# First batch of a windowed-attention and ELU kernel: masks and transposes moved to TensorE, softmax by whole heads, weights converted two halves at a time

## The chip, the cores and the metric

The kernel runs on one core of one Trainium2 chip. The metric is the device time of one execution in microseconds; the median of three runs before the change is 927.81 us (927.35 to 928.17).

## What is computed

Attention with a window, for 8 batches of 8 heads with 576 positions of 64 numbers, and then two large matrix products with an ELU between them, on 4608 tokens. Everything is float32 to the caller except that the weights arrive as float64.

```
scores = q @ k^T / 8
heads 0-3: keys 0..31 positions back        heads 4-7: 0..127 back, every 4th
attn   = exp(scores - max) / (sum + 1e-9)   out = attn @ v
x = out, all heads side by side             (4608 x 512)
h = x @ w_in        (512 x 2048)
g = h if h > 0 else exp(h) - 1
result = g @ w_out  (2048 x 512)
```

The host lays q, k and v out by pairs of heads and reorders the positions, so that each block of 32 queries sees only its own and the preceding 32 keys. So one pair of heads has 12 units (2 heads x 6) of 96 queries by 64 keys.

## The kernel before, in words

**Stages.** Attention of batch 0 runs first. Then come 9 chunks of 512 tokens. A chunk has 16 steps `f`; each multiplies by 128 columns of `w_in` (`gemm1`, L210), applies the ELU (`elu`, L221) and, two steps later (`LAG`), multiplies by 128 rows of `w_out` (`gemm2`, L237). Attention of batch `c + 1` is strewn over the steps of chunk `c` in eight portions. Chunk 0 multiplies in plain float32; from chunk 1 on each product is three matmuls of float32r parts (`xh`, `xl`, `wh`, `wl`).

**Attention of a pair of heads** (`attention`, L139): 36 small matmuls for the scores; for each of 12 units one custom VectorE (DVE) instruction that adds the mask and takes the maximum (L160) and one ScalarE (ACT) exponential with an accumulated sum (L163); on DVE the sum plus 1e-9, reciprocal and product (L164 to L166); six DVE transposes of 32x32 blocks into `pt` (L173); 12 matmuls with v; two ACT copies into `x32` (L185 or L188). In batch 0 all four pairs are first taken up to the product, then each is transposed and multiplied with v. GpSimd (POOL) does the product from batch 2 on.

**Weights** (`convert`, L81): a half is 128x512 numbers of `w_in` or `w_out`, 512 KB in float64. ACT takes the magnitude of the high words (L88), DVE does four integer operations (L89 to L96). There are 32 halves, in the order in which the steps need them; the first product of chunk 0 needs the first half, and every step needs two more. In chunk 1 the halves are split into `wh` and `wl` (`split_w`, L98). In the beginning a one-element POOL copy (L78) holds the loads of later halves back.

**What sets the order.** Matmuls keep program order on TensorE (PE), whose records all carry L109, the line of the helper `mm`. The other engines' order is drawn up by the scheduler of the tile framework, from its own model of time; an `issue_after` only puts instructions behind another one on the same engine. All loads and stores go through one queue, SyncE's (SP), in order. PSUM has 8 banks: two for `h_ps`, four for `o_ps`, two for attention (`a_ps`).

Of the kernel before, what the change touches and what calls it, by code (L numbers as in the profile page):

```python
# [9 lines left out]
F32 = mybir.dt.float32  # L10
# [7 lines left out]
WINDOW, DIL = 32, 4  # L18
# [14 lines left out]
NM = 5  # L33
AHEAD = 8
NR = NF
NE = 8
# [4 lines left out]


def _mask_of(dil, n):
    return n % 3 if dil else 3 + (n > 0)
# [3 lines left out]
def body(ctx: ExitStack, tc: tile.TileContext, q, k, v, masks, w_in, w_out, out):  # L48
# [10 lines left out]
    mask_sb = const.tile([QB, NM, 2 * G], F32, name="mask_sb")  # L59
# [3 lines left out]
    early = [wst.tile([P, 2 * DM], F32, name=f"r{NR - NE + i}") for i in range(NE)]  # L63
# [3 lines left out]
    raw, full = [None] * 2 * NF, [None] * 2 * NF  # L67
# [5 lines left out]
    def load_w(j, after=None):  # L73

        i = need[j]
        raw[i] = wst.tile([P, DM], I64, name=f"r{j % NR}")
        if after is not None:
            nc.gpsimd.tensor_copy(out=raw[i].bitcast(F32)[:QB, 0:1], in_=after[:, 0:1])  # L78
        nc.sync.dma_start(out=raw[i], in_=(w_in, w_out)[i % 2][i // 2])

    def convert(j):  # L81

        i = need[j]
        u = raw[i].bitcast(U32).rearrange("p (c two) -> p c two", two=2)
        lo, hi = u[:, :, 0], u[:, :, 1]

        e = wst.tile([P, DM], F32, name="w_e", bufs=2)
        nc.scalar.activation(out=e, in_=hi.bitcast(F32), func=AF.Abs)  # L88
        nc.vector.tensor_scalar(out=e, in0=e, scalar1=TINY, scalar2=None, op0=ALU.max)  # L89

        a = full[i] = wst.tile([P, DM], F32, name=f"a{j}")
        au, eu = a.bitcast(U32), e.bitcast(U32)
        nc.vector.tensor_scalar(out=eu, in0=eu, scalar1=0x07FFFFFF, scalar2=3, op0=ALU.bitwise_and, op1=ALU.logical_shift_left)
        nc.vector.scalar_tensor_tensor(out=eu, in0=hi, scalar=0xC0000000, in1=eu, op0=ALU.bitwise_and, op1=ALU.bitwise_or)  # L94

        nc.vector.scalar_tensor_tensor(out=au, in0=lo, scalar=29, in1=eu, op0=ALU.logical_shift_right, op1=ALU.bitwise_or)  # L96

    def split_w(j):  # L98

        i = need[j]  # L100
        if j % 2 == 0:
            split_w.pair = wst.tile([P, 2, DM], F32R, name=f"r{j // 2}")
        wh[i] = split_w.pair[:, j % 2, :]
        wl[i] = wst.tile([P, DM], F32R, name=f"a{j - 1}")
        nc.scalar.copy(out=wh[i], in_=full[i])  # L105
        nc.vector.tensor_tensor(out=wl[i], in0=full[i], in1=wh[i].bitcast(F32), op=ALU.subtract)  # L106

    def mm(*args, **kw):
        tc.keep_in_program_order(nc.tensor.matmul(*args, **kw))  # L109

    x32 = {}
    last_transpose = [None] * NPAIR
    count = [0]
    newest = [None]

    def load_pair(b, hp):
        i = b * NPAIR + hp
        if i in (2, 3):
            e = early[4 * (i - 2):]
            qt, kt = e[0][:, :S], e[1][:, :WINDOW + S]  # L120
            vt = e[2][:, :2 * NU * D].rearrange("p (u d) -> p u d", u=2 * NU)
        else:
            qt = ap.tile([P, S], F32, name="qt")
            kt = ap.tile([P, WINDOW + S], F32, name="kt")
            vt = ap.tile([P, 2 * NU, D], F32, name="vt")
        nc.sync.dma_start(out=qt, in_=q[i])
        nc.sync.dma_start(out=kt, in_=k[i])
        if i == 0:
            nc.sync.dma_start(out=mask_sb, in_=masks)
        nc.sync.dma_start(out=vt, in_=v[i])  # L130
        return qt, kt, vt

    def banks(b, hp):

        if b == 0 and hp % 3:
            return [ps_o.tile([P, TC], F32, name="o_ps") for _ in range(2)]
        return [ps_a.tile([P, TC], F32, name=f"a_ps{i}") for i in range(2)]

    def attention(b, hp, loaded):  # L139
# [3 lines left out]
        if b == 0 and hp >= 2:  # L143
            sm = early[4 * (hp - 2) + 3][:QB, :2 * NU * 2 * G].rearrange("p (u j) -> p u j", u=2 * NU)
        else:
            sm = ap.tile([QB, 2 * NU, 2 * G], F32, name="sm")
        nmx = ap.tile([QB, 2 * NU], F32, name="nmx", bufs=4)
        sums = ap.tile([QB, 2 * NU], F32, name="sums", bufs=4)
        newest[0] = nmx

        s_ps = [s[:QB, :NU * 2 * G].rearrange("p (n j) -> p n j", n=NU) for s in banks(b, hp)]
        for n in range(NU):
            for c in range(GU):
                for h in range(2):
                    hs, o = slice(h * D, (h + 1) * D), n * QB + c * G
                    mm(s_ps[h][c * G:(c + 1) * G, n, :], qt[hs, o:o + G], kt[hs, o:o + 2 * G], start=True, stop=True)
        for h in range(2):
            for n in range(NU):
                u = h * NU + n
                nc.vector.tensor_tensor_reduce(  # L160
                    out=sm[:, u, :], in0=s_ps[h][:, n, :], in1=mask_sb[:, _mask_of(dil, n), :], scale=-0.125, scalar=3.0e38,
                    op0=ALU.add, op1=ALU.min, accum_out=nmx[:, u:u + 1])
                nc.scalar.activation(out=sm[:, u, :], in_=sm[:, u, :], func=AF.Exp, bias=nmx[:, u:u + 1], scale=-1.0, accum_out=sums[:, u:u + 1])  # L163
        nc.vector.tensor_scalar(out=sums, in0=sums, scalar1=1e-9, scalar2=None, op0=ALU.add)  # L164
        nc.vector.reciprocal(out=sums, in_=sums)
        (nc.vector if b < 2 else nc.gpsimd).tensor_tensor(out=sm, in0=sm, in1=sums.unsqueeze(2).broadcast_to([QB, 2 * NU, 2 * G]), op=ALU.mult)  # L166
        yield
        tr = pt[count[0] % len(pt)]
        count[0] += 1
        for c in range(GU):  # L170
            for r in range(2):
                ks, cs, rs = slice((c + r) * G, (c + r + 1) * G), slice(c * G, (c + 1) * G), slice(r * G, (r + 1) * G)
                ins = nc.vector.transpose(out=tr[ks, :, cs], in_=sm[cs, :, rs])  # L173
        if b == 0:
            last_transpose[hp] = ins.ins
        yield
        a_ps = banks(b, hp)
        for n in range(NU):
            for h in range(2):
                u, o = h * NU + n, n % NA * QB  # L180
                mm(a_ps[n // NA][h * D:(h + 1) * D, o:o + QB], vt[:, u, :], tr[:, u, :], start=True, stop=True)
        for i in range(NU // NA):
            flat, q0, q1 = a_ps[i][:, :NA * QB], i * NA * QB, (i + 1) * NA * QB
            if dil:
                nc.scalar.copy(out=x32[b][:, hp, q0:q1], in_=flat)  # L185
            else:
                dst = x32[b][:, hp, :].rearrange("p (c u) -> p c u", c=DIL)[:, :, q0 // DIL:q1 // DIL]
                nc.scalar.copy(out=dst.rearrange("p c (s i) -> p s c i", i=G // DIL),  # L188
                               in_=flat.rearrange("p (s c i) -> p s c i", c=DIL, i=G // DIL))
        yield  # L190

    xh, xl = [None] * NC, [None] * NC

    hidden = []

    def split_x(c):
        for hp in range(NC):
# [204 lines left out]
```

## Time and profile before

| | |
|---|---|
| profiled execution | 927.86 us, of which the span from first to last instruction is 926.1 us |
| median of three runs | 927.81 us |
| busy: PE, DVE, ACT, POOL | 895.1, 539.2, 401.1, 42.2 us |
| bytes read from memory, written | 48.88 MB, 9.44 MB |

Busy time is the time in which at least one instruction of an engine was under way; PE overlaps its matmuls. A float32 matmul leaves two records, which is why 36 score matmuls are counted as 72. In a timeline row stand start, time taken, engine, line, operation, output and inputs, shapes and count, and in brackets the idle time before it with what ended it.

### The profile page before, as it was taken

The numbers are of one execution on the slowest core, as the hardware profiler recorded it, in microseconds if no ns is written. First come the engines' busy times: TensorE is split into PE (matmuls) and PEld (weight loads), VectorE is DVE, ScalarE is ACT, GpSimd is POOL, SyncE is SP. The second block draws the span as 40 slices with busy tenths as digits, with TensorE's granted clock in tenths as the row PEclk, the third lists the DMA queues.
The fourth block names the chain that finished last, engine by engine and source line by source line (L and its number), as shares of the span: only waits on it lengthen the run. The fifth ranks groups of instructions, "written<-read, shape, count | busy, mean of one in ns | idle before, by whom it ended". The sixth has DMA issues, their size and how long they took to land.

```text
span 926.1 us, 16654 instructions
## 1 busy us (share of the span) xinstructions
PE 895.1 (97%) x6400; PEld 684.9 (74%) x6400; DVE 539.2 (58%) x1652; ACT 401.1 (43%) x1281; POOL 42.2 (5%) x44
## 2 busy tenths in 40 slices
PE   3599999999999999999999999999999999999998
PEld 3344445788878887887878887888788888888886
DVE  6999985965655555655465546555655543343332
ACT  6465872543343445433453436343533432233222
POOL 1000000000000000000010001000000000000000
PEclk9999999999999999999999999999999999999999
DMA  9964010311120122111121113111300010001001
GB/s 353 352 222 151 30 43 19 99 44 45 35 87 32 43 62 73 45 44 45 49 84 31 41 35 100 45 44 35 100 18 18 1 46 1 0 1 46 1 1 46
DMA packets 23808, 59.39 MB, mean 64 GB/s; under 512 B 2640, under 2 KB 2736, under 8 KB 23728
## 3 DMA queue, kind: packets, MB, share of 16 engines
q1 hardware_dynamic: 23728, 58.33, 18.9%
q8 instruction: 50, 0.82, 0.4%
q14 instruction: 30, 0.25, 0.1%
HBM read 48.88 MB, written 9.44 MB: 63 GB/s over the span
## 4 chain that ended last, share of the span: by engine, by line
PE 85%; DVE 6%; ACT 5%; DMA 2%; issue 1%; SPq 0%; DVEq 0%; ACTq 0%
PE o_ps L109 41%; PE h_ps L109 39%; PE a_ps L109 5%; ACT sm L163 2%; DVE pt L173 1%; DVE w_e L94 1%; DMA r<-w_in 1%; ACT r L163 1%; DVE a L96 1%; DMA vt<-v 1%; ACT r L105 1%; ACT e L248 1%; DVE w_e L89 1%; DVE sm L160 0%; ACT e L223 0%
## 5 line engine op out<-in xcount | busy, mean ns | idle before, releaser
L109 PE MATMUL o_ps<-a,gh 128*128 128x512 f32 x640 | 258.4, 432 | 0.0
L223 ACT ACTIVATE e<-h_ps 128x512 f32<-128x512 f32 x144 | 85.8, 596 | 281.2 <-PE h_ps L109 274.0
L109 PE MATMUL o_ps<-r,gh 128*128 128x512 f32 x512 | 205.9, 402 | 1.3 <-ACT e L248 1.3
L109 PE MATMUL h_ps<-xh,r 128*128 128x512 f32 x512 | 200.4, 391 | 0.0
L109 PE MATMUL o_ps<-r,gl 128*128 128x512 f32 x512 | 199.7, 390 | 0.0
L109 PE MATMUL h_ps<-xl,r 128*128 128x512 f32 x512 | 199.2, 389 | 0.0
L229 DVE TENSOR_SCALAR e<-e 128x512 f32<-128x512 f32 x128 | 69.5, 543 | 182.4 <-ACT e L223 181.9
L109 PEld LDWEIGHTS o_ps<-a,gh 128*128 128x128 f32 x640 | 119.9, 188 | 45.7 <-issue 26.3
L233 ACT CAST gh<-e 128x512 fp32r<-128x512 f32 x128 | 79.5, 621 | 158.6 <-DVE e L230 158.6
L234 DVE TENSOR_TENSOR gl<-e,gh 128x512 fp32r<-128x512 f32 x128 | 88.5, 691 | 94.9 <-PE o_ps L109 83.6
L109 PE MATMUL h_ps<-xh,a 128*128 128x512 f32 x480 | 128.2, 389 | 0.0
L163 ACT ACTIVATE sm<-sm,nmx 96x64 f32<-96x64 f32 x360 | 120.0, 336 | 15.1 <-DVE nmx L160 15.0
L109 PEld LDWEIGHTS o_ps<-r,gh 128*128 128x128 f32 x512 | 96.0, 187 | 27.4 <-ACT e L248 3.7
L109 PEld LDWEIGHTS o_ps<-r,gl 128*128 128x128 f32 x512 | 96.1, 188 | 21.2
L109 PEld LDWEIGHTS h_ps<-xh,r 128*128 128x128 f32 x512 | 96.1, 188 | 20.7 <-DVE a L106 0.2
L109 PEld LDWEIGHTS h_ps<-xl,r 128*128 128x128 f32 x512 | 96.1, 188 | 20.6 <-issue 0.7
L173 DVE STREAM_TRANSPOSE pt<-sm 32x384 f32<-32x384 f32 x180 | 102.2, 568 | 14.4 <-POOL sm L166 12.2
L109 PEld LDWEIGHTS h_ps<-xh,a 128*128 128x128 f32 x480 | 90.1, 188 | 18.7
L230 DVE SCALAR_TENSOR_TENSOR e<-h_ps,e 128x512 f32<-128x512 f32 x128 | 88.4, 691 | 4.0
L163 ACT ACTIVATION_READ_ACCUMULATOR sm<-sm,nmx 96x1 f32 x360 | 67.7, 188 | 0.0
L166 POOL TENSOR_TENSOR sm<-sm,sums 96x768 f32<-96x768 f32 x24 | 36.5, 1520 | 646.4 <-ACT e L248 310.8
L109 PE MATMUL h_ps<-x,a 128*128 128x512 f32 x128 | 58.3, 600 | 1.5 <-DVE gh L227 1.5
(56 smaller groups left out, 557.7 us busy)
## 6 DMA issues: line engine op xcount, KB each, us to landing
vt<-v SPq DMA_DIRECT2D x30, 384.0 KB, 3.1
kt<-k SPq DMA_DIRECT2D x30, 304.0 KB, 4.0
qt<-q SPq DMA_DIRECT2D x30, 288.0 KB, 3.2
r<-w_in SPq DMA_DIRECT2D x16, 512.0 KB, 6.7
r<-w_out SPq DMA_DIRECT2D x16, 512.0 KB, 5.6
out<-e SPq DMA_DIRECT2D x32, 256.0 KB, 2.2
out<-xl SPq DMA_DIRECT2D x4, 256.0 KB, 2.1
r<-v SPq DMA_DIRECT2D x2, 384.0 KB, 7.8
```

What stands on the lines that cost most here:

```text
L89: nc.vector.tensor_scalar(out=e, in0=e, scalar1=TINY, scalar2=None, op0=ALU.max)
L94: nc.vector.scalar_tensor_tensor(out=eu, in0=hi, scalar=0xC0000000, in1=eu, op0=ALU.bitwise_and, op1=ALU.bitwise_or)
L96: nc.vector.scalar_tensor_tensor(out=au, in0=lo, scalar=29, in1=eu, op0=ALU.logical_shift_right, op1=ALU.bitwise_or)
L109: tc.keep_in_program_order(nc.tensor.matmul(*args, **kw))
L163: nc.scalar.activation(out=sm[:, u, :], in_=sm[:, u, :], func=AF.Exp, bias=nmx[:, u:u + 1], scale=-1.0, accum_out=sums[:, u:u + 1])
L166: (nc.vector if b < 2 else nc.gpsimd).tensor_tensor(out=sm, in0=sm, in1=sums.unsqueeze(2).broadcast_to([QB, 2 * NU, 2 * G]), op=ALU.mult)
L173: ins = nc.vector.transpose(out=tr[ks, :, cs], in_=sm[cs, :, rs])
L223: nc.scalar.activation(out=e, in_=h_ps, func=AF.Exp)
L229: nc.vector.tensor_scalar(out=e, in0=e, scalar1=1.0, scalar2=-1.0, op0=ALU.min, op1=ALU.add)
L230: nc.vector.scalar_tensor_tensor(out=e, in0=h_ps, scalar=0.0, in1=e, op0=ALU.max, op1=ALU.add)
L233: nc.scalar.copy(out=gh, in_=e)
L234: nc.vector.tensor_tensor(out=gl, in0=e, in1=gh.bitcast(F32), op=ALU.subtract)
```

## The change

- **Batch 0** gets a function of its own, `first_attention`. The mask is no longer added on DVE: a matmul of an identity matrix with the mask (96x384, `ident` and `masks`) starts each bank, and the score matmuls add to it. Maximum, subtraction and exponential each handle one head (96x384) at a time, the sum one pair (96x768). The six DVE transposes are replaced by 72 matmuls of 32x32 blocks with the identity into three PSUM banks, and four ACT copies from there into `pt`.
- **Order of the first batch:** a list of 24 phases is written out by hand and kept on PE, DVE and ACT: S scores, M maximum and exponential, P sum and product, T transposes with their copies, O outputs with their copies, A a magnitude, C a conversion; the digit is the pair. Loads have a list too: the masks first (324 KB where the masks were 120 KB), then q, k, v and the first four pairs of halves.
- **Weights** are loaded, converted and split in pairs of halves (128x1024): the same operations on twice the width, 16 times instead of 32. The magnitude is written where the result comes. Conversions keep their order among each other; from pair 2 on a magnitude stands on ACT behind the last copy of the first batch, and later behind the latest Relu. The POOL copies go.
- **Later batches:** one DVE addition of the mask (96x768, from PSUM), one maximum and one multiplication of 12 numbers take the place of the 12 custom instructions; the 12 exponentials stay. The two attention banks become one tile.

```diff
+    def first_attention(hp, loaded):
...
+        for h in range(2):
+            mm(s_ps[h], ident, mask_sb[:, int(dil), :], start=True, stop=False)
+        scores(s_ps, qt, kt, False)
+        yield
+        for h in range(2):
+            s, us = s_ps[h].rearrange("p (n j) -> p n j", n=NU), slice(h * NU, (h + 1) * NU)
+            inorder(nc.vector.tensor_reduce(out=mx[:, us], in_=s, op=ALU.max, axis=mybir.AxisListType.X))
+            inorder(nc.vector.tensor_tensor(out=sm[:, us, :], in0=s, in1=mx[:, us].unsqueeze(2).broadcast_to([QB, NU, 2 * G]), op=ALU.subtract))
+            inorder(nc.scalar.activation(out=sm[:, us, :], in_=sm[:, us, :], func=AF.Exp, scale=0.125))
+        yield
+        inorder(nc.vector.tensor_reduce(out=sums, in_=sm, op=ALU.add, axis=mybir.AxisListType.X))
+        last_step[hp] = normalise(nc.vector, sm, sums, inorder).ins
+        yield
...
+        t_ps = [ps_o.tile([P, TC], F32, name="o_ps") for _ in range(GU)]
+        for u in range(2 * NU):
+            for r in range(2):
+                for c in range(GU):
+                    ks, cs, rs = slice((c + r) * G, (c + r + 1) * G), slice(c * G, (c + 1) * G), slice(r * G, (r + 1) * G)
+                    mm(t_ps[c][ks, u * G:(u + 1) * G], sm[cs, u, rs], ident[cs, cs], start=True, stop=True)
+        for c, ks in ((0, slice(0, 2 * G)), (1, slice(G, 2 * G)), (1, slice(2 * G, 3 * G)), (2, slice(2 * G, 4 * G))):
+            inorder(nc.scalar.copy(out=tr[ks, :, c * G:(c + 1) * G], in_=t_ps[c][ks, :2 * NU * G].rearrange("p (u q) -> p u q", u=2 * NU)))
+        yield
+        yield outputs(0, hp, [(ps_o.tile([P, TC], F32, name="o_ps"), 0, 0, NU - 1), (t_ps[0], 2 * NU * G, NU - 1, NU)], vt, tr, inorder)
...
+    for what in "qk0 qk1 v0 w0 qk2 v1 qk3 v2 v3 w1 w2 w3".split():
...
+    for what in "S0 S1 M0 M1 A0 S2 S3 P0 M2 T0 O0 P1 M3 T1 O1 A1 P2 T2 O2 P3 T3 O3 C0 C1".split():
+        i = int(what[1])
+        if what[0] == "A":
+            inorder(magnitude(i))
+        elif what[0] == "C":
+            last_conversion = convert(i, inorder)
+        else:
+            last_copy = next(its[i])
...
-            while c == 0 and ready < min(2 * NF, 2 * f + AHEAD):
-
-                with tc.issue_after(last_transpose[{0: 1, 2: 2}.get(ready, NPAIR - 1)]):
-                    convert(ready)
-                if ready + NR < 2 * NF:
+            while c == 0 and ready < min(NF, f + AHEAD):
+                with tc.issue_after(below[-1] if below else last_copy.ins):
+                    magnitude(ready)
+                with tc.issue_after(last_conversion.ins):
+                    last_conversion = convert(ready)
+                if ready + NR < NF:
                     load_w(ready + NR)
                 ready += 1
```

More of the change, by code (lines that the diff above doesn't have):

```diff
@@ L64, in body @@
     for z in pt:
         nc.gpsimd.memset(z, 0.0)
-    raw, full = [None] * 2 * NF, [None] * 2 * NF
+    raw, full2, full = [None] * NF, [None] * NF, [None] * 2 * NF
     need = sorted(range(2 * NF), key=lambda i: i // 2 + (i % 2) * (LAG + 0.5))
     wh, wl = [None] * 2 * NF, [None] * 2 * NF
[L73 to L106, printed above, removed]
-    def mm(*args, **kw):
-        tc.keep_in_program_order(nc.tensor.matmul(*args, **kw))
+    def inorder(ins):
+        tc.keep_in_program_order(ins)
+        return ins
@@ L126, in load_pair, with scores @@
         nc.sync.dma_start(out=qt, in_=q[i])
         nc.sync.dma_start(out=kt, in_=k[i])
-        if i == 0:
-            nc.sync.dma_start(out=mask_sb, in_=masks)
         nc.sync.dma_start(out=vt, in_=v[i])
         return qt, kt, vt
[L133 to L139, printed above, removed]
-        dil = hp >= NPAIR // 2
-        qt, kt, vt = loaded
[L143 to L151, printed above, removed]
+    def scores(s_ps, qt, kt, start):
```

215 lines of the change are left out of this document (129 added, 86 removed).

## Prediction

> **What bounds the kernel now.** I read the page first, then busy time by stages, then the timeline of PE, then the groups of the first 45 us. The page's first two parts and busy time in stages (us; busy time and count of each engine, granted clock, DMA share, GB/s):
>
> ```profile
> PE 895.1 (97%) x6400; PEld 684.9 (74%) x6400; DVE 539.2 (58%) x1652; ACT 401.1 (43%) x1281; POOL 42.2 (5%) x44
> PE   3599999999999999999999999999999999999998
> ...
> 0.00:39.60 39.60, 15.15 (x384) 13.12 (x384) 30.43 (x146) 22.11 (x111) 5.28 (x19) 1.00 0.95 357
> 39.60:60.00 20.40, 19.76 (x169) 9.17 (x172) 20.10 (x63) 14.19 (x42) 0.42 (x1) 1.00 0.84 286
> 100.00:110.00 10.00, 9.19 (x43) 4.17 (x42) 9.66 (x20) 6.83 (x24) 0.00 (x0) 1.00 0.15 39
> 160.00:926.10 766.10, 760.98 (x5375) 615.79 (x5373) 404.09 (x1223) 304.66 (x967) 36.49 (x24) 1.00 0.13 42
> ```
>
> From 39.60 us on PE has almost no gap: 0.64 us up to 60, 0.81 us in 100 to 110. Its work there is large matmuls that the change leaves alone. So time can change in three ways: the moment of the first large matmul, the stalls behind it, and the rate at which PE runs just after it. The 39.60 us before it are the stage to cost: PE is busy for 15.15 us, DVE for 30.43.
>
> PE's timeline of that stage with DVE's last transposes, the chain's row of a later product, and one more burst:
>
> ```profile
> 4.65 1.52 PE L109 MATMUL a_ps<-kt,qt 64*32 64x64 f32 x72 [4.65 <-DMA kt<-k]
> 16.49 1.92 PE L109 MATMUL a_ps<-r,r 64*32 64x64 f32 x72 [4.11 <-DMA r<-k]
> 20.84 2.19 PE L109 MATMUL a_ps<-pt,vt 128*64 128x96 f32 x24 [2.43 <-DVE nmx L160]
> 25.06 2.19 PE L109 MATMUL o_ps<-pt,vt 128*64 128x96 f32 x24 [2.03 <-issue]
> 32.26 2.19 PE L109 MATMUL o_ps<-pt,r 128*64 128x96 f32 x24 [5.01 <-DVE pt L173]
> 33.91 3.47 DVE L173 STREAM_TRANSPOSE pt<-r 32x384 f32<-32x384 f32 x6
> 37.49 2.19 PE L109 MATMUL a_ps<-pt,r 128*64 128x96 f32 x24 [3.04 <-issue]
> 39.60 7.79 PE L109 MATMUL h_ps<-x,a 128*128 128x512 f32 x16
> 47.32 0.97 PE L109 MATMUL a_ps<-kt,qt 64*32 64x64 f32 x72
> 48.93 3.70 PE L109 MATMUL h_ps<-x,a 128*128 128x512 f32 x8 [0.64 <-DVE gh L227]
> ...
> 52.63 3.43 PE o_ps L109 x8
> ...
> 74.26 1.21 PE L109 MATMUL a_ps<-pt,vt 128*64 128x96 f32 x24
> ```
>
> Three things are to be seen. The last scores wait for their keys until 16.49. After them the head is set by ACT's exponentials and then DVE's transposes: the outputs of pair 2 wait 5.01 us for `pt`. And every small burst up to 39.6 is slow: scores take 1.52 us where they later take 0.97, outputs 2.19 where they later take 1.21. The large matmuls show when that ends: 16 records would take 2 x 3.43 = 6.86 us at the later rate (3.43 is the chain's row at 52.63) and took 7.79, so about two of them were still slow; the full rate came near 41.2, some 3.7 us after PE began to work without a break at 37.49. The granted clock says 1.00 all the while and does not show this.
>
> **What goes.** The rows of the first 45 us, the chain's row of the exponentials, and ACT's pair of copies:
>
> ```profile
> 19.31 7.96 ACT r L163 x48
> 27.17 0.67 ACT L188 COPY x<-a_ps 128x288 f32<-128x288 f32 x2
> L163 ACT ACTIVATE sm<-sm,nmx 96x64 f32<-96x64 f32 x24 | 8.0, 333 | 4.5 <-DVE nmx L160 4.5
> L173 DVE STREAM_TRANSPOSE pt<-sm 32x384 f32<-32x384 f32 x12 | 6.8, 568 | 0.2
> L166 DVE TENSOR_TENSOR sm<-sm,sums 96x768 f32<-96x768 f32 x2 | 1.9, 958 | 0.0
> L164 DVE TENSOR_SCALAR sums<-sums 96x12 f32<-96x12 f32 x4 | 0.7, 164 | 0.1
> L165 DVE RECIPROCAL sums<-sums 96x12 f32<-96x12 f32 x4 | 0.9, 220 | 0.0
> L89 DVE TENSOR_SCALAR w_e<-w_e 128x512 f32<-128x512 f32 x6 | 2.6, 425 | 0.1
> L94 DVE SCALAR_TENSOR_TENSOR w_e<-r,w_e 128x512 uint32<-128x512 uint32 x5 | 3.4, 683 | 0.0
> ```
>
> DVE loses 4 x 6 transposes of 0.568 = 13.6 us, ACT 48 exponentials at 7.96 / 24 = 0.33 us = 15.9 us. The POOL copies go at no gain; POOL is 5% busy.
>
> **What DVE does instead.** Two rows give the cost of a number, and others the sizes between:
>
> ```profile
> L207 DVE TENSOR_TENSOR xl<-x,xh 128x448 fp32r<-128x448 f32 x8 | 5.0, 619 | 2.1 <-ACT xh L206 2.1
> L207 DVE TENSOR_TENSOR xl<-x,xh 128x64 fp32r<-128x64 f32 x8 | 1.7, 218 | 0.2 <-ACT xh L206 0.2
> ```
>
> That is (619 - 218) / 384 = 1.04 ns a number and 0.15 us fixed, so a subtraction of 96x384 takes 0.55 us. No row shows a maximum or sum along a row. Bounds: a tensor-scalar instruction (0.425 for 512, so 0.32 for 384) and the transposes (0.568 for 384); I take 0.55, and 0.95 for 768, near the two-input rows. M is then 2 x (0.55 + 0.55) = 2.2 us a pair, P 0.95 + 0.16 + 0.22 + 0.96 = 2.3, both 4.5, for four pairs 18 us. M starts near 8 us: masks there at about 4 (q and k of pair 0 let PE start at 4.65, now the masks come first), their matmuls 2.6 (below) and scores 1.52; with some 3 us of waiting for scores P3 ends near 29. A conversion of two halves is 2 x 0.70 + 2 x 1.22 = 3.8 us (each twice its row less 0.15 fixed), where two single ones take 4 x 0.425 + 4 x 0.683 = 4.4 (two operations are like L89, two like L94); C0 ends near 33, C1 near 37. I show below that neither is what PE waits for.
>
> **What becomes the path.** PE keeps program order, T0 O0 T1 O1 T2 O2 T3 O3, and T0 stands behind S3. T fills three of four `o_ps` banks and O the fourth, so T of the next pair also waits for the copies of O. T, its four copies, O and its copies thus run one after the other, four times.
>
> *Start.* S3 needs q and k of pair 3. Sizes and the rate:
>
> ```profile
> kt<-k SPq DMA_DIRECT2D x30, 304.0 KB, 4.0
> qt<-q SPq DMA_DIRECT2D x30, 288.0 KB, 3.2
> vt<-v SPq DMA_DIRECT2D x30, 384.0 KB, 3.1
> r<-w_in SPq DMA_DIRECT2D x16, 512.0 KB, 6.7
> mask_sb<-masks SPq DMA_DIRECT2D x1, 120.0 KB, 3.5
> 10.00:20.00 10.00, 3.50 (x149) 2.84 (x144) 9.52 (x66) 6.57 (x35) 1.45 (x7) 1.00 1.03 407
> ```
>
> Up to and with those keys the SP queue carried 4 x 592 + 3 x 384 + 120 + 512 = 4152 KB; in the new list it is 4 x 592 + 2 x 384 + 324 + 1024 = 4484 KB. 332 KB more at 407 GB/s is 0.8 us: the keys come at 17.3 instead of 16.49. The masks of S3 can run before. P0 is over near 15 by the DVE sum (8.1 + 2 x 2.2 + 2.3), so S3's scores decide: T0 starts at 17.3 + 0.97 = 18.3.
>
> Two rows more, of a copy and of a later batch's masks:
>
> ```profile
> L248 ACT COPY e<-o_ps 128x512 f32<-128x512 f32 x32 | 17.2, 578 | 4.5 <-DMA out<-e 4.3
> L160 DVE CUSTOM_DVE_ANT_0 sm<-a_ps,mask_sb 96x64 f32<-96x64 f32 x348 | 52.6, 215 | 6.2 <-PE a_ps L109 6.2
> ```
>
> *One round, at PE's full rate.* T is 72 matmuls, 144 records, with as many columns in all as the 72 records of a pair's scores (72 x 32 = 36 x 64): between 0.97 us, if columns count, and 1.94, if records count; I take the middle, 1.45, since neither is nearer. A copy of 288 numbers takes 0.38 and two take 0.67, so one follows the other after 0.29; by size (0.578 for 512) 384 numbers take 0.475 and four 4 x 0.475 - 3 x 0.1 = 1.6. O is 1.21. Its copies (480 and 96 numbers) leave about 0.5 after PE's end, since the first starts before. Three hand-overs of 0.1 (pair 3's transposes ended at 33.91 + 3.47 = 37.38 and PE began at 37.49). One round: 1.45 + 1.6 + 1.21 + 0.5 + 0.3 = 5.06. Four rounds without the last copies, which three quarters of the first product cover: 20.2 - 0.6 = 19.6. First large matmul: 18.3 + 19.6 = 37.9, against 39.60: 1.7 us earlier. DVE's P3 (29) stands before T3 at 18.3 + 15.2 = 33.5; C0 (33) is 5 us early. That cover gone, each us that DVE is late costs one.
>
> *Which rate.* From about 4 us, when the masks land, the new kernel's PE has 4 records of 384 columns a pair and 72 of scores, for two pairs without a pause: masks at the slow rate 4 x 0.64 (0.86 x 384/512; 0.86 is twice 3.43/8) = 2.6, scores 1.52, and the second pair behind, over 6 us. 3.7 us sufficed at 41.2. After that no pause is as long as the 4.11 us before 16.49: the longest I find is about three us before S2 (its masks are done near 11.6, its keys come 976 KB or 2.5 us before those of pair 3), then 1.7 in each round. So I take the full rate, but the trace shows no burst after a pause of 1 to 4 us following a full-rate stretch; the half rate is a rival below. [...]
>
> *Behind the start.* At the full rate the first product doesn't lose 7.79 - 6.86 = 0.9 us. The stalls of 0.64 and 0.81 came from DVE, which was behind with conversions (20.10 busy of 20.40). Now two pairs are converted before PE starts and the third is needed 4 x 3.43 + 0.97 = 14.7 us later; but magnitudes 2 and 3 stand on ACT behind the last copy of O3, so DVE is idle from C1 (37) to about 39.5 and has 14 x 3.8 us left beside PE's 110. I put the stalls at 0.5, between 0 and 3: 0.95 gained.
>
> *Hidden:* in later batches a pair costs DVE 0.95 + 0.95 + 0.16 = 2.1 us instead of 12 x 52.6 / 348 = 1.8; DVE has 404 us of work in the last 766, and outputs follow their scores by two portions. One tile for two banks and ACT's and DVE's longer splits (about 1.2 us) are covered by that and by the two steps of lag.
>
> **Sum.** -1.7 - 0.9 - 0.95 = -3.55 us. 926.1 - 3.55 + 1.76 (the profiled run's 927.86 less its span) = 924.3 us; that run stands 0.05 over the median of 927.81.
>
> **Rivals.** *Slower: PE stays at half rate (0.22).* For it: the bursts at 20.84 and 25.06 filled half of the time and stayed slow. Round: T 2.3 (1.52 to 3.04), O 2.19, so 2.3 + 1.6 + 2.19 + 0.8 = 6.89; start 17.3 + 1.52 + 27.6 - 0.6 = 45.8, 6.2 later; the 0.9 stays, the stalls still gain 0.95: 933.1 us. It decides from a round of about 5.5 us, where PE starts no earlier.
>
> *Slower: transposes cost by the record, more than the scores' 13.5 ns (0.10).* At 1.52 / 72 = 21 ns T is 3.0 us even at full rate, 6.2 us more in four rounds: 930.5. Against it: 0.97 / 72. [...]
>
> *No change: DVE takes the gain back (0.18).* DVE's `gh`, queued behind conversions of 3.8 us, stalls the third product, as it did for 0.64, now for 2 to 3 us; 924.3 + 2.5 = 926.8. For it: longer conversions that start later; against it: DVE is no longer behind when PE starts.
>
> **Numbers.** Forecast 0.50. What can be told from no change is about 0.2%, 1.86 us. Faster 0.50; same 0.18; slower 0.22 + 0.10 = 0.32. Low end: T at 0.97 (-1.9), keys at 16.4 (-0.9), no stall (-0.5), 921.0, rounded down to 920.5; high end the half-rate case, 933.5. Some 0.15 is left out. The forecast's own range is 921 to 926.
>
> **What would show it.** Keys of pair 3 near 17.3; T of 1.0 to 1.9 us and O of 1.2 in the first batch (2.2 means the half rate); four rounds near 5 us; the first large matmul near 38 and 16 of its records in 6.9 us; no wait of PE for `pt` over 2 us, none for conversions. It is wrong if T waits for DVE, or if DVE's late `gh` holds PE in 40 to 60.

## The result, and the profile after

962.65 us (median of four, 960.75 to 963.92) beside 927.99 for the kernel before: ratio 1.0373, 95% interval 1.0354 to 1.0391. I had forecast 924.3 within 920.5 to 933.5; no rival came near either. The profiled execution took 962.97 us with a span of 960.7, 35.1 more than the profiled 927.86. Its page says less than its waits. Three lines of the page (busy time; the granted clock in 40 slices; packets, MB and share of the queue that brings instructions), then what PE waited for (sum, times, longest):

```profile
PE 913.7 (95%) x6992; PEld 693.8 (72%) x6992; DVE 522.8 (54%) x884; ACT 393.0 (41%) x1177; POOL 41.4 (4%) x30
...
PEclk9599999999999999999999999999999999999999
...
q8 instruction: 55, 0.90, 0.4%
```

```profile
PE o_ps L76 <- issue: 11.0, 4, 4.5
PE a_ps L76 <- ACT x L160: 10.2, 14, 2.5
PE a_ps L76 <- ACT x L157: 7.0, 14, 0.5
PE o_ps L76 <- ACT pt L215: 5.6, 3, 1.9
```

DVE and ACT have less to do, as the change meant, and DVE holds PE nowhere. PE has two new kinds of wait. One lies in the later batches (L160 and L157 are the copies of `outputs`): 28 times, 17.2 us. The other is "issue" in the first batch, where PE waits for nothing that the profile shows. PE's timeline of the first batch (L215 copies the transposes out of PSUM):

```profile
4.28 2.88 PE L76 MATMUL a_ps<-masks_sb 96*96 96x384 f32 x4 [4.28 <-DMA masks_sb<-masks]
7.08 1.37 PE L76 MATMUL a_ps<-kt,qt 64*32 64x64 f32 x72
8.38 1.53 PE L76 MATMUL h_ps<-masks_sb 96*96 96x384 f32 x4
9.84 0.97 PE L76 MATMUL h_ps<-kt,qt 64*32 64x64 f32 x72
10.83 1.50 PE L76 MATMUL a_ps<-masks_sb 96*96 96x384 f32 x4
12.73 0.87 PE L76 MATMUL a_ps<-r 64*32 64x64 f32 x65 [0.39 <-DMA r<-k]
14.66 0.31 PE L76 MATMUL a_ps<-r 64*32 64x64 f32 x7 [1.06 <-issue]
14.90 1.53 PE L76 MATMUL h_ps<-masks_sb 96*96 96x384 f32 x4
16.55 0.96 PE L76 MATMUL h_ps<-r 64*32 64x64 f32 x72
17.44 0.57 PE L76 MATMUL o_ps<-masks_sb,sm 32*32 32x32 f32 x43
22.52 1.27 PE L76 MATMUL o_ps<-masks_sb,sm 32*32 32x32 f32 x101 [4.51 <-issue]
25.76 2.19 PE L76 MATMUL o_ps<-pt,vt 128*64 128x96 f32 x24 [1.97 <-issue]
27.88 0.31 PE L76 MATMUL o_ps<-masks_sb,sm 32*32 32x32 f32 x2
28.35 1.54 PE L76 MATMUL o_ps<-masks_sb,sm 32*32 32x32 f32 x128 [0.17 <-issue]
34.28 0.37 PE L76 MATMUL o_ps<-masks_sb,sm 32*32 32x32 f32 x14 [4.38 <-issue]
36.54 2.19 PE L76 MATMUL o_ps<-pt,vt 128*64 128x96 f32 x24 [1.90 <-ACT pt L215]
38.66 2.10 PE L76 MATMUL o_ps<-masks_sb,r 32*32 32x32 f32 x144
42.60 2.19 PE L76 MATMUL o_ps<-pt,r 128*64 128x96 f32 x24 [1.84 <-ACT pt L215]
```

The first large matmul follows at 50.77, against 39.60 before. From there to the end of the span it takes 960.7 - 50.77 = 909.9 us, against 926.1 - 39.60 = 886.5. So 35.1 = 11.2 at the start, 23.4 behind it, and 0.5 around the span.

*Behind the start.* In `outputs` six matmuls go into one half of the tile `a_ps`, then a copy of that half, then six into the other half. PE's rows of one such place, and ACT's:

```profile
84.83 0.72 PE L76 MATMUL a_ps<-pt,vt 128*64 128x96 f32 x12
88.09 0.72 PE L76 MATMUL a_ps<-pt,vt 128*64 128x96 f32 x12 [2.55 <-ACT x L160]
```

```profile
87.18 0.58 ACT L276 ACTIVATE e<-h_ps 128x512 f32<-128x512 f32 x1
87.66 0.38 ACT L160 COPY x<-a_ps 128x288 f32<-128x288 f32 x1
```

The second six, in another bank, wait for ACT's copy of the first, and that copy stood behind other work on ACT. Every output of batches 1 to 7 is cut so: 17.2 us of waits, and 28 x (0.72 + 0.72 - 1.21) = 6.4 us because two bursts of 12 records take longer than one of 24 (1.21 us before); together 23.6. The first batch calls the same function with two different tiles in place of the two halves of one, and there the 24 records of an output run without a gap (2.19 us in the timeline above). So it is the order of emission together with the one tile that makes PE wait.

### The profile page after: what moved, and what is told of

The parts are those of the page before. It is cut to its first block, busy times and chain, and to the rows that moved or that the text cites. A ratio compares the mean times of both kernels' runs of the same rounds, so it can differ in the third digit from the quotient of the medians.

```text
span 960.7 us, 16849 instructions
## 1 busy us (share of the span) xinstructions
PE 913.7 (95%) x6992; PEld 693.8 (72%) x6992; DVE 522.8 (54%) x884; ACT 393.0 (41%) x1177; POOL 41.4 (4%) x30
## 4 chain that ended last, share of the span: by engine, by line
PE 87%; ACT 6%; DVE 4%; issue 2%; DMA 1%; SPq 0%; ACTq 0%
PE o_ps L76 43%; PE h_ps L76 39%; PE a_ps L76 5%; ACT sm L233 2%; ACT e L276 2%; DMA r<-k 1%; ACT x L157 1%; DVE a L107 1%; ACT x L160 1%; DVE a L105 1%; DVE pt L239 1%; ACT pt L215 1%; DVE a L102 0%; SPq L334 0%; DVE nmx L230 0%
## 5 line engine op out<-in xcount | busy, mean ns | idle before, releaser
L282 DVE TENSOR_SCALAR e<-e 128x512 f32<-128x512 f32 x128 | 59.1, 462 | 179.3 <-ACT e L276 178.3
L233 ACT ACTIVATE sm<-sm,nmx 96x64 f32<-96x64 f32 x336 | 112.0, 335 | 34.4 <-DVE nmx L231 34.4
L76 PE MATMUL h_ps<-xh,a 128*128 128x512 f32 x448 | 119.7, 389 | 0.0
L239 DVE STREAM_TRANSPOSE pt<-sm 32x384 f32<-32x384 f32 x168 | 95.5, 568 | 12.8 <-POOL sm L167 10.9
L76 PEld LDWEIGHTS h_ps<-xh,a 128*128 128x128 f32 x448 | 84.1, 188 | 17.5
L167 POOL TENSOR_TENSOR sm<-sm,sums 96x768 f32<-96x768 f32 x24 | 39.2, 1632 | 716.1 <-ACT e L276 334.3
L233 ACT ACTIVATION_READ_ACCUMULATOR sm<-sm,nmx 96x1 f32 x336 | 62.9, 187 | 0.0
```

The source lines that it names most:

```text
L76: inorder(nc.tensor.matmul(*args, **kw))
L167: return keep(eng.tensor_tensor(out=sm, in0=sm, in1=sums.unsqueeze(2).broadcast_to([QB, 2 * NU, 2 * G]), op=ALU.mult))
L282: nc.vector.tensor_scalar(out=e, in0=e, scalar1=1.0, scalar2=-1.0, op0=ALU.min, op1=ALU.add)
```

## The experiments

Changes are to the kernel after unless another is named.

**e1: all twelve matmuls of an output before its copies.**

```diff
         for a_ps, col, n0, n1 in places:
             for n in range(n0, n1):
                 ...
+        for a_ps, col, n0, n1 in places:
             flat, q0, q1 = a_ps[:, col:col + (n1 - n0) * QB], n0 * QB, n1 * QB
```

> The changed kernel, but the twelve output matmuls of a pair all stand ahead of the two copies, instead of six, a copy, six, a copy. Theory: in later batches the second six wait for the copy of the first six because both banks are one tile; 17.1 us of PE waits for that copy and 28 second starts of 0.23 us go, so about 962.7 - 23.5 = 939 us. Rival: ACT's reading holds PE's writing in PSUM, whatever the order; then the first copy only moves behind and the time stays within 3 us of 962.7.

939.97 us, ratio to before 1.0122 (1.0107 to 1.0137). An output is one row again:

```profile
82.64 1.21 PE L76 MATMUL a_ps<-pt,vt 128*64 128x96 f32 x24
```

The profiled execution takes 935.8 - 48.55 = 887.25 us of span from the first large matmul, against 886.5 before. So the order in `outputs` is nearly the whole loss behind the start, and the rival is refuted; what is left, 9 us, lies in the head. The 0.75 us between 887.25 and 886.5 hide two changes: PE's waits for DVE's `gh`, 1.5 us before, are gone, and its waits for ACT's copies of a chunk's output (L302, L248 before) grew from 1.3 to 3.3 us. Whether two tiles in the order of the change would do as well in the later batches was not run.

**e4: e1, with the first batch's transposes on DVE as before.** The four copies go with the matmuls.

```diff
-                    mm(t_ps[c][ks, u * G:(u + 1) * G], sm[cs, u, rs], ident[cs, cs], start=True, stop=True)
...
+                inorder(nc.vector.transpose(out=tr[ks, :, cs], in_=sm[cs, :, rs]))
```

> Output matmuls ahead of their copies, and the first batch's transposes back on DVE (six of 0.57 us a pair) with no copies from PSUM; masks on PE, maxima and exponentials of whole heads, pairs of halves stay. Theory: with 48 records a round in place of 336 PE no longer outruns its instructions; DVE becomes the path with 4 x 8.0 us from 8.5 on and the first conversion behind, first large matmul near 45, time near 934 us. Rival, that PE's stalls come with the loads: stalls of about 4 us between 18 and 34 us stay on PE.

935.9 us, ratio 1.0086 (1.0071 to 1.0101). No stall by "issue" inside a burst is left, but DVE now does everything: PE waits 5.69 us for DVE's transposes before the outputs of pair 1, and 1.75 us for its conversion before the first product. So putting the transposes on PE costs 4 us net with its stalls, by the medians, and something else costs the rest.

**e9: e4, with mask, maximum and exponential by blocks of 96x64 as before.**

```diff
-        for h in range(2):
-            mm(s_ps[h], ident, mask_sb[:, int(dil), :], start=True, stop=False)
...
+                inorder(nc.vector.tensor_tensor_reduce(out=sm[:, u, :], in0=s_ps[h][:, js], in1=mask_sb[:, int(dil), js], scale=-0.125, scalar=3.0e38, op0=ALU.add, op1=ALU.min, accum_out=mx[:, u:u + 1]))
+                inorder(nc.scalar.activation(out=sm[:, u, :], in_=sm[:, u, :], func=AF.Exp, bias=mx[:, u:u + 1], scale=-1.0, accum_out=sums[:, u:u + 1]))
```

> As e4 (transposes of the first batch on DVE, outputs in the new order), but the first batch's maxima and exponentials are again taken a block of 96 queries at a time, as before the change: no masks on PE, and the sums come out of the exponentials. The theory (DVE sets the start of e4, and whole heads are not what costs): by the rows of the kernel before, a block costs DVE 0.216 + 0.078 and ACT 0.333 + 0.186 us, so a pair 3.5 and 6.2 us against 2.2 and 1.05 with whole heads; DVE saves the 0.94 of the sum and loses 1.3, and ACT with 4 x 6.2 = 25 us comes onto the path: first large matmul at 46 to 48 us, total 936 to 938 us. The rival (whole-head maxima, subtraction and sum are the loss, since the fused pass did mask, scale and maximum in one): first large matmul before 44 us, total 934 us or less.

932.36 us, ratio 1.0044 (1.0031 to 1.0057): the rival was right. The first large matmul, in e4 and then in e9:

```profile
46.10 9.92 PE L76 MATMUL h_ps<-x,a 128*128 128x512 f32 x16 [1.75 <-DVE a L107]
```

```profile
41.61 9.80 PE L76 MATMUL h_ps<-x,a 128*128 128x512 f32 x16 [1.75 <-DVE a L107]
```

The error of the theory is seen in DVE's rows of e9:

```profile
8.35 0.22 DVE L199 CUSTOM_DVE_ANT_0 sm<-a_ps,masks_sb 96x64 f32<-96x64 f32 x1 [8.35 <-PE a_ps L76]
8.50 0.08 DVE L199 DVE_READ_ACCUMULATOR2_ANT nmx<- 96x1 f32 x1
8.50 0.21 DVE L199 CUSTOM_DVE_ANT_0 sm<-a_ps,masks_sb 96x64 f32<-96x64 f32 x1
```

The next block starts 0.15 us after the last: the durations 0.22 and 0.08 overlap and must not be added. Twelve blocks cost DVE 1.75 us with mask, scale and maximum done, and the sum comes from ACT. Whole heads cost 2 x (0.547 + 0.554) and 0.94 for the sum, 3.1 us. That is 1.4 us a pair, 5.5 in all, and 4.5 of it shows at the start. The edit also takes the masks off PE, but in e4 PE had waited 3.8 us or more before every output, so the masks did not set that start. In the changed kernel itself PE waits for DVE nowhere; there the whole heads cost nothing that can be seen, and their price shows once the transposes are back on DVE.

**e10: e4, with the first two conversions a half at a time** (four operations on 128x512, twice).

```diff
-O3 C0 C1
+O3 C00 C01 C10 C11
+            lo, hi, a = lo[:, ts], hi[:, ts], a[:, ts]
```

> As e4, but each of the two conversions of the first batch is done a half at a time (four operations on 128x512, twice), so that the first product waits for half a pair. The theory (the first product of e4 waits for DVE's conversion, and only for that): DVE reaches the needed half 1.9 us sooner, the wait of 1.75 us at the first large matmul goes: 44.3 us, total 934.2 us. The rival (the first product is held by the last outputs and by PE's rate anyway): first large matmul as in e4, total 935.9 us, or up to 0.5 more for the eight added operations.

935.2 us, ratio 1.0073 (1.0061 to 1.0085): 0.7 less than e4 where 1.7 was expected. The start came to 44.56, 1.54 sooner, so the wait for the conversion is gone. How much of it the total keeps is not settled: the medians differ by 0.7 us, the two profiled executions by 2.1, and the four runs of e4 lie 2.3 us apart.

**e11: e10, pairs 0 and 1 transposed on DVE, 2 and 3 on PE.**

```diff
+        if hp in (0, 1):
...
+                    inorder(nc.vector.transpose(out=tr[ks, :, cs], in_=sm[cs, :, rs]))
```

> As e10, but only pairs 0 and 1 are transposed on DVE; pairs 2 and 3 are transposed on PE as in the change, and pair 2's maxima come after pair 0's outputs. The theory (e4 is held by DVE's sum of work, e1 by PE's supply of instructions and half rate, so a share for each is better than either): DVE from 9 us has 4 x 4.5 + 2 x 3.4 + 1.9 = 26.7 us, done by 36; after P3 at 34 follow T 2.1, copies 1.8 and O 2.2: first large matmul at 40 to 41 us, total 930 to 931 us. The rival (the supply still stalls T2 and T3, 2.6 to 4.5 us each, though PE has been slower up to there): first large matmul at 43 to 46 us, total 933 to 936 us.

936.25 us, ratio 1.0074 (1.0062 to 1.0086); first large matmul at 46.74. That is a little beyond the rival's range (46 and 936), and only half by its reason: T2 stalls for 2.06 us by "issue" and T3 does not, but T, copies and O of the last two pairs also run one after the other with nothing between.

**e12: e9 with e10, the masks loaded after the first q and k, and an order in which DVE does not wait for ACT.**

```diff
-S0 S1 M0 M1 A0 S2 S3 P0 M2 T0 O0 P1 M3 T1 O1 A1 P2 T2 O2 P3 T3 O3 C0 C1
+S0 S1 M0 M1 S2 S3 P0 T0 M2 A0 M3 O0 P1 T1 O1 A1 P2 T2 O2 C00 P3 T3 O3 C01 C10 C11
```

> e9 with the half-wise conversion of e10, the masks loaded after the first queries and keys as in the kernel before, and the order by hand turned so that DVE does not wait for ACT: T0 ahead of M2, M3 ahead of P1, the first half of C0 ahead of P3. What remains of the change is that order, the conversion by pairs after the first two, and the outputs on one tile with their copies behind all matmuls. The theory (PE's masks and transposes and the whole heads are all that cost at the start, and ACT's 4 x 6.2 = 25 us for 48 exponentials are what is left): ACT starts at 6.3, ends at 32.5; P3 1.3, T3 3.5, O3 2.2 follow: first large matmul at 39 to 40 us, total 927.5 to 929.5 us, the same as the kernel before. The rival (the conversion by pairs is late too, since DVE has all its conversions after the start): first large matmul as early, but waits of PE for DVE after it, total 930.5 us or more.

929.54 us (929.16 to 930.64), ratio 1.0015 (1.0006 to 1.0024); first large matmul at 39.69 against 39.60. With PE's masks, PE's transposes and the whole heads out of the first batch, and the cut outputs out of the later ones, the change is nearly a tie. No version here beat the kernel before.

**The stalls by "issue": counts.** Add the matmul records in the timeline of the changed kernel up to the first stall by "issue" (two bursts of 4 and 72, then 4 and 65): 221. Up to the next ones it is 7 + 4 + 72 + 43 = 126, 101 + 24 + 2 = 127, and 128 more. Each record has one weight load, so these stalls lie 252 to 256 instructions apart. The page counts 55 transfers of 0.90 MB in all on a queue named "instruction", 16.4 KB each, and PE and PEld have 2 x 6992 = 13984 instructions, 54.6 times 256. The kernel before has 2 x 6400, 50.0 times 256, and the page has

```profile
q8 instruction: 50, 0.82, 0.4%
```

**e6: e1, with 21 small matmuls (42 records) ahead of pair 2's masks.**

```diff
+        if hp == 2:
+            for _ in range(21):
+                mm(s_ps[0][:, :G], ident, mask_sb[:, 0, :G], start=True, stop=True)
```

> Output matmuls ahead of their copies, and 21 small matmuls (84 records on PE and its weight loads) more ahead of the masks of pair 2, where PE waits for its keys anyway. They write a part of a bank that the masks overwrite. Theory: stalls sit at fixed counts of instructions, so they stay at records 695, 949 and 1205 from the first: the first at the very start of T0 (record 693), the third 84 records sooner than the end of T1, at its first half. Rival: they belong to T0 and T1 and their data; then they stay at T0's 43rd and T1's 130th record, 84 records later in the count.

941.7 us, ratio 1.0154 (1.0134 to 1.0174). PE's rows of its first transposes:

```profile
20.23 0.21 PE L76 MATMUL o_ps<-masks_sb,sm 32*32 32x32 f32 x1
22.89 1.27 PE L76 MATMUL o_ps<-masks_sb,sm 32*32 32x32 f32 x128 [2.45 <-issue]
28.82 0.42 PE L76 MATMUL o_ps<-masks_sb,sm 32*32 32x32 f32 x15 [4.65 <-issue]
```

The stall is after 347 records as before, now one record into T0 instead of 43, and the next 128 later. It belongs to the count, not to the data. The packets of the queue "instruction" say what PE waits for. In the changed kernel the first four end at 13.20, 21.22, 27.12 and 32.98 us, and PE goes on after its four stalls at 14.66, 22.52, 28.35 and 34.28, each time 1.2 to 1.5 us later. After 730 and 858 records, where the next two blocks begin, there is no stall: their packets had ended 3.0 and 2.4 us before. So PE waits for blocks of 256 instructions.

**e5, e13, e14, e15: what slows that supply?** e5 is e1 with the loads of weights held by a POOL copy into the tile, which needs pair 3's maxima.

```diff
+            nc.gpsimd.tensor_copy(out=raw[k].rearrange("p t c -> p (t c)").bitcast(F32)[:QB, 0:1], in_=after[:, 0:1])
```

> Output matmuls ahead of their copies; all loads of weights (w0 to w3 and what follows them) are held until the maxima of pair 3, by a POOL copy of one number, and the two magnitudes stand later on ACT. Theory: a block of PE's 256 instructions is asked for when the block before it is entered and comes 4.4 us later on a quiet DMA queue and 5.9 to 7.9 us later beside loads. T0 starts near 16; its stall at record 695 shrinks from 2.6 to under 1.5 us, first large matmul 3 to 6 us earlier than 48.6, time near 935 us. Rival: the supply is slow whatever the loads; then the stall in T0 stays 2.6 us or grows, and the time falls by no more than the 1.5 us by which T0 starts earlier.

938.67 us, ratio 1.0122 (1.0106 to 1.0137), stalls 3.18 and 4.38. Alone that would say "not the loads". But the DMA share in 17 to 21 us was still 1.03: the copy touched only the first half of a pair, and other loads filled the queue. e13 holds all loads behind the first batch's until pair 3's sums; e14 lets the first pair of weights go early; both still miss the second halves. e15 is e14 with both halves held.

```diff
-            nc.gpsimd.tensor_copy(out=raw[k].rearrange("p t c -> p (t c)").bitcast(F32)[:QB, 0:1], in_=after[:, 0:1])
+            for t in range(2):
+                nc.gpsimd.tensor_copy(out=raw[k][:, t, :].bitcast(F32)[:QB, 0:1], in_=after[:, 0:1])
```

> As e1, but every load behind the first batch's own q, k and v (weights, the second batch's first pair) is held by a POOL copy until pair 3's sums are done, so that the DMA engines are idle while the first three transposes run. In e5 they were not: other loads had taken the place of the held ones, and the DMA share stayed at 1.03. Theory (the supply of 256 instructions in 5.9 us is slow because its 16 KB transfers share the DMA engines with the loads): the DMA share falls below 0.3 from about 14 us on, the stalls after 347 and after 602 matmul records go or stay under 0.7 us each, first large matmul near 42 to 44 us, unless it waits for the late weights (landing near 30, magnitude 1.1, conversion 3.85). The rival (the supply has its own pace whatever the DMA engines do): DMA share as low, but stalls of about 3 and 4.4 us at the same two counts, first large matmul at 48 to 49 us.

> As e13, but the first pair of halves (1 MB) keeps its early place in the list, so that the first product need not wait for its weights. Theory (loads slow the supply): the DMA engines are full until about 16 us and idle after, the stall after 347 records is between that of e13 and the 2.6 us of e1, that after 602 is gone, first large matmul at 42 to 45 us, total 934 to 936 us unless later weights are late. The rival: stalls and start as in e1 (48.6 us), total 940 us or more.

> As e14, but both halves of each held pair wait (in e5, e13 and e14 only the first half was touched by the POOL copy, so five loads of second halves ran from 10 to 21 us and kept the DMA share at 1.02 there). Theory (loads slow the supply of instructions): DMA idle from about 15 us to P3, the stall after 347 records falls below 1 us as that after 602 did in e13 and e14 (0.34 and 0.35), first large matmul at 43 to 44 us, total 932 to 933.5 us, unless the weights, released near 30 us, are late. The rival (the supply starts with two blocks and the third needs its own time, loads or not): stall after 347 records still 3 us or more, first large matmul at 46 to 48 us.

941.22, 936.18 and 932.9 us; ratios 1.0145 (1.013 to 1.016), 1.0089 (1.0072 to 1.0106), 1.0056 (1.0039 to 1.0072). In e13 the first product waits 5.54 us for its conversion, as its weights come late. The stall after 602 records in e1 with the window inside it, then both stalls of e15 with windows ahead of the second (the last three columns are granted clock, DMA share and GB/s):

```profile
32.06 0.37 PE L76 MATMUL o_ps<-masks_sb,sm 32*32 32x32 f32 x14 [4.38 <-issue]
```

```profile
28.00:30.00 2.00, 0.00 (x0) 0.00 (x0) 1.93 (x5) 0.00 (x0) 0.00 (x0) 0.50 1.05 427
```

```profile
19.59 1.06 PE L76 MATMUL o_ps<-masks_sb,sm 32*32 32x32 f32 x101 [2.05 <-issue]
...
26.86 0.37 PE L76 MATMUL o_ps<-masks_sb,sm 32*32 32x32 f32 x14 [0.19 <-issue]
```

```profile
17.00:21.00 4.00, 1.59 (x146) 1.39 (x144) 3.86 (x8) 0.81 (x2) 0.00 (x0) 1.00 0.04 10
21.00:25.00 4.00, 2.38 (x28) 2.11 (x28) 2.96 (x6) 1.97 (x6) 0.00 (x0) 0.56 0.01 4
```

With idle DMA engines (share 0.02 in 25 to 29 us of e15, too) the stall after 602 records falls from 4.38 to 0.19 us (0.34 and 0.35 in e13 and e14). Where the loads came back (share 1.03 in 37 to 41 us of e13 and e15), a stall appears that e1 does not have: 1.26 and 0.59 us inside T3. So the loads slow the supply of instructions. The packets show where: the one for the stall after 602 records takes 0.97 us in e1 and 0.96 in e15, but in e1 it starts 3.6 us after PE has gone on into the block before it (26.14 and 29.75), in e15 at the same moment (both near 24.8). The stall after 347 records is settled in part only. In e15 it lasts 2.05 us under a DMA share of 0.04; its packet starts 2.9 us after PE enters the block before it, at 14.25 us, when the loads still filled the engines (share 1.03 in 10 to 14 us, 0.74 in 14 to 17). In e1, e13 and e14 the loads go on (share 1.03 in 10 to 20 us, 1.02 and 1.04 in 17 to 21), the packet starts 3.4, 3.9 and 5.3 us after, and the stall is 2.64, 3.18 and 4.51; why these three differ stays open. The expectation of e5 has a block asked for when the one before it is entered, and gives it 4.4 us on a quiet queue: both were my estimates. For the stall after 602 records of e15 the packet does start at that moment; no run shows the 4.4 us. A wait for a block lasted up to 4.51 us in the changed kernel, where small matmuls met full DMA engines (share 1.03 in 17 to 22 us), and up to 4.65 in e6.

**e2, e3 and e7: fewer, larger transposes.** e2 takes blocks of 32x64 where the window allows, 48 matmuls instead of 72, both shapes in turn; e3 is e2 with e1; e7 is e1 with all 24 of one shape before the 24 of the other.

```diff
+            for c, r0, r1 in ((0, 0, 2), (1, 0, 1), (2, 0, 2), (1, 1, 2)):
+                ks, cs, rs = slice((c + r0) * G, (c + r1) * G), slice(c * G, (c + 1) * G), slice(r0 * G, r1 * G)
```

> The changed kernel, but two of the six blocks of a unit are transposed together where their place allows it: 48 transposing matmuls a pair instead of 72, 192 records on PE and its weight loads instead of 288. Theory: PE's instructions come in blocks of some 256 and a block takes about 5.9 us here, so PE stalls at every block boundary that it reaches sooner. The boundaries stay near records 443, 695, 949 and 1205 counted from the first; the stall at 695 stays (4.5 us), the one at 1205 (4.4 us) goes, the first large matmul comes near 45.5 instead of 50.8, the time falls by about 5 to some 957.5 us. Rival: the stalls belong to data or loads at fixed moments (18.0 and 29.9 us); then both stay in T0 and T1 and the time falls by under 2 us.

> Both edits together: output matmuls ahead of their copies, and 48 transposing matmuls a pair. If the two causes are apart, the savings add: 962.7 - 23.5 - 5 = 934 us, still 6 above the kernel before. If the output gaps and the stalls have one cause, it comes out above 945.

> Output matmuls ahead of their copies, and 48 transposing matmuls a pair as before, but first all 24 of 32x64 and then all 24 of 32x32, so that the shape changes once a pair instead of 24 times. Theory: the change of shape made T 14.2 us; grouped, T takes 1.3 to 2.9 us. With 240 records a round instead of 336 the stall at record 695 stays, that at 1205 goes: 4 us less than the 940.0 of the same kernel with 72 transposes, near 936 us. Rival: a 32x64 transpose is slow by itself, some 0.15 us a record; then T stays above 7 us and the time above 955.

1000.8, 978.12 and 939.72 us; ratios 1.0773 (1.075 to 1.0797), 1.0544 (1.0528 to 1.056), 1.013 (1.0115 to 1.0145). A pair's transposes in e2 and in e7:

```profile
19.97 14.15 PE L76 MATMUL o_ps<-masks_sb,sm 32*64 32x32 f32 x96
```

```profile
27.20 4.19 PE L76 MATMUL o_ps<-masks_sb,sm 32*64 32x32 f32 x96
```

A miss: shapes in turn cost 147 ns a record, shapes in groups 44, the original 2.10 / 144 = 15; the granted clock was 0.50 for the first (20 to 30 us of e2) and the last (36 to 50 us of the changed kernel), and e7's outputs on both sides of the row take 2.19 us as the original's do. Why 96 grouped records still take twice as long as the original 144, and shapes in turn 3.4 times as long as grouped ones, is not shown. The gain of e1's order is the same beside these transposes (e2 less e3: 22.7 us) as without them (after less e1: 22.7).

**e8 and e16: the clock.** e8 is e5 with two unread 96x512 matmuls behind each pair's transposes, to shorten PE's pauses; e16 is e15 with the same.

```diff
+        for _ in range(2):
+            mm(filler[:QB, 0, :], ident, masks_sb[:, :TC], start=True, stop=True)
```

> As with the held loads, and two dense matmuls of 96x512 whose result nobody reads stand behind each pair's transposes on PE, where it waits for the copies. Theory: the array falls to half rate in the rounds because PE does too little in a window; with the fillers (1.7 us each round at full rate) it stays at full rate from about 9 us on, O takes 1.2 us instead of 2.2 and T 1.3 instead of 2.1, which is 1.9 us a round or up to 7 us, near 930 us. Rival: the rate falls all the same (a stall comes first), the fillers take 3.4 us each and delay O by 1.5 us in four rounds: some 941 us.

> As e15 with the two unread 96x512 matmuls of e8 behind each pair's transposes. Theory (what is left of the head is half rate): outputs at 1.21 us instead of 2.19 and the first 16 records in 7.1 us instead of 7.7, 2 to 4 us from the start of the first product, total 929 to 931 us. The rival (the pause of 1.9 us for the copies and the weights, released as late as before, set the pace): 931.5 us or more.

937.18 us, ratio 1.0102 (1.0085 to 1.0119), and 936.96, ratio 1.0101 (1.0085 to 1.0117). In e8 the outputs of pairs 2 and 3 took 1.21 and 1.31 us instead of 2.19, and the first 16 records 7.13 us instead of e5's 7.70, for 1.5 us in all, as the fillers take 1.96 to 3.73 us themselves. Of pair 3's transposes 140 records took 1.39 us, as long as 140 of pair 2's at 32.71 us of e16, where the granted clock was 1.00 (29 to 37 us):

```profile
44.39 1.39 PE L76 MATMUL o_ps<-masks_sb,r 32*32 32x32 f32 x140 [0.31 <-ACT x L162]
```

In e16 the fillers made it 4 us slower than e15; the first large matmul came at 47.07 instead of 44.22. As a remedy it fails. That the half rate is there without long pauses is seen in e15, whose longest pause after 17 us is 2.05 us (granted clock 0.56 in 21 to 25 us in the row above, 0.50 from there to 45 us), and in a window of e2, where PE is busy nine tenths of the time:

```profile
60.00:90.00 30.00, 27.17 (x204) 21.63 (x205) 1.10 (x2) 4.52 (x11) 0.00 (x0) 0.50 0.23 71
```

## Why the prediction was wrong

**The step that failed most** is in "Hidden": "One tile for two banks ... covered by that and by the two steps of lag." The part behind the start was 23.4 of the 35.1 us, and e1, which changes that order alone, takes 22.7 off. I asked whether a slower engine would be covered, and not whether the order of emission on one tile puts an ACT copy between PE's own matmuls. The two steps of lag protect the reader of the output, not PE, which keeps program order.

**The start** was off by 50.77 - 37.9 = 12.9 us:

- *T0's place* was right: 17.44 for 18.3. S3's scores ran at 16.55, straight behind their masks.
- *A supply of instructions* had no term: 4.51 + 4.38 = 8.9 us inside T0 and T1. The shorter stage before had no such rows, as its PE had 384 records in 39.6 us. That the stalls belong to counts is shown by e6 and the packets; that loads lengthen the one in T1, after 602 records, by e13 to e15.
- *Full rate* was wrong. It was reached (scores in 0.97, masks in 1.5), and was lost at about 22 us (granted clock 0.82 in 21 to 22 us, 0.50 from 22), inside the stall of 4.51 us. (The views put 1.00 where the trace has no entry of the clock, and its first one is at 7.98 us, at 40.95 before the change; so the 1.00 beside the slow bursts ahead of that is not a measurement.) I took pauses under four microseconds as safe; e15 shows half rate with pauses of at most 2.05. No run shows by what rule the full rate ends or comes back; that too little work in a window ends it (the theory of e8) was a guess, and e2's window, at half rate with PE 27.17 of 30 us busy, disagrees, as far as busy records can tell. A round took 42.60 - 36.54 = 6.06 instead of 5.06, some 4 us in four.
- *The rest* of the 12.9: T0 came 0.9 us sooner; the 0.6 us that I had taken off behind O3 did not come off, and a third stall took 0.17. So 8.9 + 4.0 + 0.6 + 0.2 - 0.9 = 12.8, but for rounding the whole.
- *T* took 2.10 us at half rate. For the full rate my 1.45 was right: e8's 140 records in 1.39 us make 1.43 for 144. It was the middle of two bounds, taken because neither was nearer, so that is luck. By the record it is 1390 / 140 = 9.9 ns, by the matmul, of two records, 19.9.
- *Copies*: PE's wait was 1.84 us for 1.6 plus hand-overs; the four together took 1.81, each 0.47, with less overlap than I took from a pair of copies.

**Behind the start** I had also counted 0.9 us for a first product at full rate and 0.95 for stalls. The first did not come: the clock was at half rate, and the 16 records took 7.90 us instead of 6.86. The second came, as the 1.5 us of waits for `gh` went, and was taken back by 2 us more of waits for the output's copies.

**Behind DVE's sum.** M 2.2, P 2.3 and conversion 3.8 us came out as worked out (0.547, 0.554, 0.94; 0.69, 0.69, 1.23, 1.23). DVE was early, as predicted, and the rival that it takes the gain back is refuted. But I did not set the price of the replaced instructions beside it. "Hidden" has that price for the later batches, 12 x 52.6 / 348 = 1.8 us, and in the first batch whole heads take 3.1. e9 shows the fused blocks cheaper by 1.4 us a pair, so DVE lost where I counted only ACT's saving; it matters in the versions in which PE waits for DVE.

**The rivals.** *Half rate* did come, and its point of decision was right (rounds over 5.5 us start later than before); at 933.1 us, alone, it would have been within the range. *Transposes by the record* at 21 ns is refuted: T would take 3.0 us at full rate, where e8 shows 1.4. No rival had the cut outputs or the supply.

## What to carry to other kernels

Where two halves of a PSUM tile are filled and emptied in turn, look at the order of emission first: matmuls of both, then copies of both, took 22.7 us off here. Before moving work to PE as many small matmuls in a stage in which loads fill the DMA engines, count its instructions in blocks of 256, and price the bursts at half rate too: small matmuls that filled nine tenths of PE's time (27.17 of 30 us in e2) did not bring the full rate back here. Price a fused instruction by the distance between successive starts (0.15 us in e9), not by the sum of its rows (0.22 and 0.08).

## What the runs showed of the hardware

- In the changed kernel PE waits for its instructions in blocks of 256 (its stalls lie 252 to 256 instructions apart) and goes on 1.2 to 1.5 us after a block's packet of 16.4 KB has ended. Where its small matmuls run under a DMA share of 1.03, a wait lasts up to 4.51 us, and up to 4.65 in e6; in e15, under shares of 0.04 and 0.02, 2.05 and 0.19 us.
- Two tile shapes in turn cost 147 ns a record at a granted clock of 0.50 (e2); in two groups 44 ns (e7).
- The granted clock stays at 0.50 in a stream of small matmuls with PE busy 27.17 of 30 us (e2). With two 96x512 matmuls a round, outputs take 1.21 us in place of the changed kernel's 2.19 in two of the four rounds of e16, and 1.21 and 1.31 in two of e8.
- In the changed kernel a maximum along rows of 96x384 takes 0.547 us and a sum of 96x768 0.94, as long as the two-input operations of the same sizes (0.554 and 0.95).
- In e9 a fused block of 96x64 (mask, scale and maximum) starts 0.15 us after the one before, though its two rows last 0.22 and 0.08 us.
